# A gated mix of memory attention and a SwiGLU feed-forward block: stacks filled earlier, and part of the second half's input operands kept in DRAM

## The chip, the cores and the metric

The kernel runs on one core of one Trainium2 chip. Its time is the device time of one execution in microseconds (us). Several executions are timed, and the median is given; one more execution is recorded by the hardware profiler. The core's engines run side by side, each with an instruction stream of its own: TensorE (PE, with PEld for its weight loads), VectorE (DVE), ScalarE (ACT), GpSimd (POOL), and SyncE (SP), which issues nearly all DMAs.

## The reference

For x of 2048 tokens and D = 576 features the kernel computes one output:

```python
g = sigmoid((x * gate_w).sum(-1))
a = attention_with_memory(x, wq, wk, wv, wo, beta)   # 32 heads of 18, 4 segments of 512 tokens
b = (silu(x @ w_gate) * (x @ w_up)) @ w_down         # F = 4608
out = g * a + (1 - g) * b
```

In attention each segment of 512 tokens has causal softmax attention within itself, and a second part that reads a memory matrix per head, summed up over the segments before it: `num / den` of phi(q) with M and z, where phi(t) is t + 1 above zero and exp(t) below. The two parts are mixed by sigmoid(beta) of the head. Everything is float32 in the reference.

## The kernel before, in words

**Precision.** A float32 operand is split into a high part in TensorE's rounded format (`split`, L104: ScalarE copies, VectorE subtracts) and a low part, the remainder. A product is then three matmuls: high·high, high·low, low·high. An operand of two 128-row blocks is one tile of 128 × 2 × 512 floats, 512 KB, with high and low side by side.

**Stage 1, projections (L269 to L562).** Over four segments s of 512 tokens: nine chains for q and k (`qk`), then eight value steps n = 0 to 7 (`v_step`, with `mem_step` for the memory part). The x of a segment lives in tiles named `xo` plus `xs`; `xs_of[s]` holds the four split x tiles and the remainder of 64 rows. q and k go to DRAM (`stk`), the values to `vd`, the memory part to `med`. Those stores are first put into the list `late`; `flush` issues them some steps afterwards (L304, L527, L541, L558). In segment 3 the x sums of the feed-forward block's first half are made too (`first_load`, `first_sum`, `first_split`), and in its value steps the weight operands of unit 0 (`w_make`, list `start`).

**Feed-forward block, two halves.** Each half handles 1024 tokens as two column blocks (`HALF`: segments 2 and 3, then 0 and 1). A half has 36 units f of 128 rows of F. The gate and up products of a unit are combined into seven products of sums, as in Strassen's scheme: `seven(t, w[j], XO[j], ...)` with j = 0 to 6, weight operands w[j] and x operands XO[j]. XO[0], XO[3] and XO[5] are split parts of x itself; XO[1], XO[2], XO[4] and XO[6] are split sums or differences of x parts. `SLOT` says which `xo` tile pair holds operand j. Each j has two tiles, z = 0 and 1.

In half 0, `w_make` makes the weight operands (sums on POOL at L232, high parts on ScalarE at L236, low parts on VectorE at L239) and stores them to DRAM (`wc`, `rc`; L249 and L252). In half 1 `w_fetch` loads them back. There are only six operand tiles (pool `wop`): one comes free when its product is done and, in half 0, its store has landed.

**Order of the work.** The program is written in the order in which it is to run; each engine executes its own part in that order and waits where a tile is not ready. A unit has eight `tick`s; each calls `beat` (L870), which runs the front entry of the list `due` (deferred loads, sums, splits and stores, put there by `defer(k, ...)`, k beats ahead), then a number of down groups (`down_group`: products with w_down, added to `ya` on VectorE at L787), and, by a credit counter, steps of the attention generator `att_gen`. Between the halves ten extra beats (`BREAK`) run with the down groups of the last unit.

**Attention.** It works through 64 units u (two heads of a segment each), one after another, beside the feed-forward block. For each, `stack_load` (L179) loads stacked q and k rows from `stk` into `qst` and `kst` (four tiles each, in turn by u % 4), `s_bank` finds row maxima (L619, L626), `m_tr` transposes them to `mt`, stored to `mxd`; `row_load` (L195) loads three rows of it back into `qst`, and `t_bank` (L659, then the exponential on ScalarE, L663) uses them. Rows of kst beyond what is loaded must hold −1 (memsets at L602 and L604). The tiles qst, kst, mb and others lie in the pool `kp`, which is opened at L596, after stage 1, over memory that stage 1 used; the first write to it waits for the last reader of that memory.

**The second half's x.** `x_second` (L889) lists what prepares XO and XS of half 1: per z four loads of x parts into `raw` tiles (256 KB each, q = 0 to 3), four sums on POOL (`x_sum`, L153) and seven splits, plus the remainder of 64 rows for two blocks, loaded and split. Its numbers are beats counted from the first tick of the last unit of half 0 (f = 35): 0 to 7 are that unit's ticks, 8 on are the break's beats.

**Queues.** SP issues its DMAs strictly in program order. In the built program each DMA also waits until the eighth DMA before it has landed, since eight semaphores are used in turn. So a DMA whose data are late holds up all that stand behind it on SP.

Of the kernel before, what the change touches and what calls it, by code (L numbers as in the profile page):

```python
# [12 lines left out]
F32 = mybir.dt.float32  # L13
F32R = mybir.dt.float32r
BF = mybir.dt.bfloat16
# [5 lines left out]
P = 128  # L21
# [30 lines left out]
def f32(ap):  # L52
    return ap.bitcast(F32)
# [3 lines left out]
def gated_mix(ctx, tc, xT, wf, wd, wv, wo, beta, cmask, ident, bmask, out):  # L57
# [11 lines left out]
    mxd = dram.tile([2 * NB, 3, 8, P], BF, name="mxd")  # L69
    wc = dram.tile([FT, 7, P, 4 * P], F32, name="wc")  # L70
    rc = dram.tile([FT, 2, P, 2 * P], F32, name="rc")
    dc = dram.tile([FT, P, 2 * D], F32, name="dc")
    ffd = dram.tile([8, P, D], F32, name="ffd")
    atd = dram.tile([16, P, D], F32, name="atd")
# [29 lines left out]
    def split(hi, lo, src):  # L104
        nc.scalar.activation(hi, src, AF.Copy)  # L105
        nc.vector.tensor_sub(lo, src, f32(hi))  # L106
# [39 lines left out]
    def x_split(x, kt, raw):  # L146
# [2 lines left out]
            split(xk[kt][:, 0], xk[kt][:, 1], raw)  # L149
        else:  # L150
            xs_split(xs, raw)

    def x_sum(j, c, d, e, g):  # L153
        if j == 1:
            nc.gpsimd.tensor_sub(c, d, c)
        elif j == 2:
            nc.gpsimd.tensor_sub(c, g, c)
        elif j == 4:
            nc.gpsimd.tensor_sub(d, g, d)
        elif j == 6:  # L160
            nc.gpsimd.tensor_sub(e, e, c)

    spare = [(j, z) for j in (2, 3, 4) for z in range(2)]
    turns = iter(spare + [(j, z) for j in (5, 6) for z in range(2)] + 20 * spare)
# [104 lines left out]
    with ExitStack() as st:  # L269
        qst_ = ExitStack()  # L270
        qp = pool(qst_, "qp", 1, side="right")
        vp = pool(st, "vp", 1)
        sp = pool(st, "sp", 2)
        qw = []
        for m in range(5):
            qw.append([[qp.tile([P, NT, P], F32R, name=f"{z}{m}{u}") for u in range(2 if m < 4 else 1)] for z in ("qhi", "qlo")])
        vw = [vp.tile([P, 2, NT, 290], F32R, name=f"vw{hf}") for hf in range(2)]
        vf = vp.tile([P, 4, H, E], F32, name="vf")
        vps = [vp.tile([P, 4, 16, 3, E], BF, name=f"vps{hf}") for hf in range(2)]
        bm = vp.tile([P, NT, MW], BF, name="bm")  # L280
# [216 lines left out]
        for s in range(NSEG):  # L497
            upd = upd_gen(s - 1) if s else None
            casts = []
            for n, (m, u) in enumerate(chains):  # L500
                mid = []
                if s == 0:
                    for z in loads.get(n, []):
                        z()
                    if n + 3 < 9:
                        mid.append(lambda n=n: q_split(*chains[n + 3]))
                    if n in halves:
                        mid.append(lambda n=n: v_split(*halves[n]))
                if s == 1 and n < 3:
                    cast = masks(*((0, 3), (3, NT), (0, 0))[n])  # L510
                    casts.append(cast)
                if s == 1 and 3 <= n < 6:
                    mid.append(casts[n - 3])
                if (s, n) == (1, 7):
                    mid.append(betas)
                if s == 3:
                    if 2 <= n < 6:
                        first_load(n - 2)
                    for j, z in FSUM.get(n, []):
                        mid.append(lambda j=j, z=z: first_sum(j, z))  # L520
                    for j, z in FSPLIT.get(n, []):
                        mid.append(lambda j=j, z=z: first_split(j, z))
                if s < 3:
                    for kt in ((0, 1), (2, 3), (4,))[n - 6] if s == 0 and n > 5 else (n - 4,) if s and n > 3 else ():
                        raws["x", kt] = x_load(s + 1, kt)
                qk(s, m, u, mid)
                flush(2)  # L527
                if upd is not None and n > 0:
                    next(upd, None)
            if s == 3:  # L530
                qst_.close()
                rp = pool(ctx, "rp", 4, side="right")
                wop = pool(ctx, "wop", 6, side="right")
                for z in range(2):
                    for j, b, kt in ((0, 2, z), (3, 2, 2 + z), (5, 3, 2 + z)):
                        XO[j][z] = xs_of[b][0][kt]
                wraw_of[0] = [w_load(0, u) for u in range(2)]
                start = w_make(0)
            for n in range(8):
                hf, i = divmod(n, 4)  # L540
                flush()  # L541
                v_step(s, hf, i)
                if s:
                    mem_step(s, n // 2, n % 2)
                if s < 3:
                    if n == 0:
                        xs_of[s + 1] = x_tiles(s + 1)
                    if 1 <= n < 6:
                        x_split(xs_of[s + 1], n - 1, raws["x", n - 1])
                else:  # L550
                    if n == 4:
                        wraw_of[1] = [w_load(1, u) for u in range(2)]
                    if n < 2:
                        first_sum(6, n)
                    for _ in range((0, 0, 2, 3, 3, 3, 3, 3)[n]):
                        if start[0][0] < 8:
                            start.pop(0)[1]()
# [7 lines left out]
    with ExitStack() as st:  # L565
# [12 lines left out]
        def row_tile():  # L578
            return rw.tile([P, L], F32, name="row")
# [15 lines left out]

        kp = pool(ast, "kp", 2, side="right")  # L596
        ap = pool(ast, "ap", 2, side="right")
        for i in range(NST):
            qst.append(kp.tile([P, 2, L], BF, name=f"qst{i}", bufs=1))
            kst.append(kp.tile([P, 2, L], BF, name=f"kst{i}", bufs=1))  # L600
            if i:
                defer(2 * i - 1, lambda i=i: nc.gpsimd.memset(kst[i], -1.0))  # L602
            else:
                nc.gpsimd.memset(kst[i], -1.0)  # L604
        for i in range(2):
            mbs.append(kp.tile([P, P], F32, name=f"mb{i}", bufs=1))
            nc.gpsimd.memset(mbs[i], 0.0)
        for pr in range(2):
            stack_load(0, pr)
        SPLAN = [[(0, 0, 3)], [(0, 1, 3)], [(384, 0, 0), (0, 0, 2)], [(384, 1, 0), (0, 1, 2)], [(0, 0, 1), (256, 1, 1)]]  # L610

        def s_bank(u, n):
# [100 lines left out]
        def att_gen():  # L713
            N = 10 * NB
            for tau in range(N + TL + VL + 4):
# [4 lines left out]
                    nc.sync.dma_start(mxd[u - 1].rearrange("z q n -> q z n"), mts.pop(u - 1))  # L720
                if n == 0 and 2 <= u <= 2 * NB + 1:
                    row_load(u - 2)
                if n in (2, 3) and u + 1 < 2 * NB:
                    stack_load(u + 1, n - 2)
                z = tau - TL - VL - 1
                if z % 20 == 0 and 0 <= z < N and z // 20 + 1 < 4 * NSEG:
# [161 lines left out]

        def x_second(new, xs):  # L889
            r = {}  # L890

            def load(z, q):
                b, kt = ((0, z), (1, z), (0, 2 + z), (1, 2 + z))[q]
                r[z, q] = raw_tile()[:, :L]
                nc.sync.dma_start(r[z, q], xT[HALF[1][b], :, kt])

            def total(z, j):
                x_sum(j, *(r[z, q] for q in range(4)))

            def parts(z, j):  # L900
                new[j][z] = x_slot(SLOT[j], z)
                split(new[j][z][:, 0], new[j][z][:, 1], r[z, (0, 0, 0, 2, 1, 3, 2)[j]])

            def rest_load(b):
                r[b] = row_tile()
                nc.sync.dma_start(r[b], xT[HALF[1][b], :, 4])

            def rest(b):
                xs[b] = xs_tile()
                xs_split(xs[b], r[b])  # L910

            todo = []
# [26 lines left out]
        for pos, (half, f) in enumerate(seq):  # L939
# [176 lines left out]
```

## Time and profile before

| what | value |
|---|---|
| median of 3 runs | 1901.21 us (1895.81 to 1901.78) |
| the profiled execution | 1899.41 us, of which its span 1897.60 |
| mean granted TensorE clock | 0.993 of full |
| TensorE busy | 1822.3 us |
| VectorE, ScalarE, GpSimd busy | 1222.2, 961.5, 856.1 us |
| DMA traffic | 330.83 MB, mean 174 GB/s |

Stages in the trace: projections to 224 us, half 0 from there to about 1000, the break to 1034, half 1 to about 1800, the output product to 1898. The profile's tables are read like this: a group's line gives the source line, the engine, the operation and the tiles (out<-in); an instruction's line in a timeline begins with its start and its duration in us, and ends in square brackets with the time its engine sat idle before it and what ended that. A window's line gives the stretch, its length, then the busy time of PE, PEld, DVE, ACT and POOL with their numbers of instructions, the granted clock, the busy share of the DMA engines and GB/s. A wait's line names the waiting instruction, what it waited for, us in total, how many times, and the longest.

### The profile page before, as it was taken

The page shows a single profiled execution, that of the slowest core. Times are in us where ns is not written, and L with a number is a line of the kernel's source. Part 1 is how long each engine was busy: PE and PEld are TensorE (multiplying, and loading weights), DVE is VectorE, ACT ScalarE, POOL GpSimd, SP SyncE. Part 2 cuts the span into 40 slices and gives each one's busy share as a digit, 9 for nine tenths or more (in the row PEclk, how much of TensorE's full clock was granted, in tenths as well). Part 3 has the DMA queues.
Part 4 walks back from the last instruction along what each step waited for, and adds up shares of the span by engine and source line. Part 5 has one row for each costly group of instructions (what it writes and reads, how often), then busy time and mean ns, then how long its engine had stood idle before and what let it go on. Part 6 is the DMA issues. An engine that isn't in the chain of part 4 may idle for free.

```text
span 1897.6 us, 36543 instructions
## 1 busy us (share of the span) xinstructions
PE 1822.3 (96%) x12508; PEld 1546.4 (81%) x12508; DVE 1222.2 (64%) x3034; ACT 961.5 (51%) x1786; POOL 856.1 (45%) x1246
## 2 busy tenths in 40 slices
PE   8999989999999999999998999999999999999999
PEld 7889867877877887887787788878878878888899
DVE  5555666777767777876777565656556555655455
ACT  7666545466456556645654544554454444355311
POOL 3323622455544555555455444445454444445121
PEclk9999989999999999999999999999999999999999
DMA  6444485466456447645646644554554354445544
GB/s 226 157 143 167 156 277 193 147 230 205 140 195 230 158 161 239 212 153 188 221 156 209 205 150 119 186 160 129 160 180 149 122 177 148 140 151 156 191 149 138
DMA packets 204457, 330.83 MB, mean 174 GB/s; under 512 B 38192, under 2 KB 95664, under 8 KB 204272
## 3 DMA queue, kind: packets, MB, share of 16 engines
q1 hardware_dynamic: 204272, 328.50, 53.0%
q8 instruction: 100, 1.64, 0.4%
q14 instruction: 85, 0.70, 0.1%
HBM read 194.33 MB, written 134.09 MB: 173 GB/s over the span
## 4 chain that ended last, share of the span: by engine, by line
PE 77%; DVE 6%; DMA 6%; ACT 5%; issue 4%; SPq 2%; POOL 1%; DVEq 0%; ACTq 0%; POOLq 0%
PE bank L927 26%; PE bank L782 23%; PE bank L128 11%; PE bank L933 5%; PE bank L619 3%; PE bank L659 3%; PE bank L688 2%; PE bank L690 1%; ACT L663 1%; PE bank L369 1%; DMA draw<-in_wd_dram 1%; ACT pe L663 1%; ACT L1001 1%; PE bank L415 1%; SPq L189 1%
## 5 line engine op out<-in xcount | busy, mean ns | idle before, releaser
L738 POOL TENSOR_TENSOR p<-pe,p 128x512 f16<-128x512 f32 x320 | 372.8, 1165 | 692.0 <-DVE p L736 608.0
L782 PE MATMUL bank<-dw,hh 128*128 128x288 f32 x2304 | 484.4, 303 | 18.6 <-DVE ya L787 12.9
L782 PEld LDWEIGHTS bank<-dw,hh 128*128 128x128 f32 x2304 | 380.3, 190 | 41.4 <-DVE ya L787 19.7
L663 ACT ACTIVATE pe<-bank 128x512 f32<-128x512 f32 x320 | 191.0, 597 | 339.2 <-PE bank L659 301.2
L782 PE MATMUL bank<-dw,hl 128*128 128x288 f32 x1152 | 341.4, 296 | 1.5 <-DVE hl L106 1.5
L787 DVE TENSOR_TENSOR ya<-bank,ya 128x288 f32<-128x288 f32 x352 | 159.7, 455 | 229.4 <-PE bank L782 227.3
L626 DVE CUSTOM_DVE_ANT_0 scr<-bank,cm 128x512 bf16<-128x512 f32 (+3 forms) x512 | 246.9, 482 | 18.6 <-PE bank L619 11.8
L782 PEld LDWEIGHTS bank<-dw,hl 128*128 128x128 f32 x1152 | 218.1, 189 | 1.9 <-DVE hl L106 1.9
L659 PE MATMUL bank<-qst,kst 111*128 111x512 bf16 (+3 forms) x512 | 152.1, 305 | 0.0
L736 DVE CAST p<-pe 128x512 f16<-128x512 f32 x320 | 150.1, 469 | 1.0 <-POOL pe L671 0.9
L671 POOL TENSOR_SCALAR_AFFINE_SELECT pe<-pe 128x256 f32<-128x256 f32 (+1 forms) x320 | 135.9, 425 | 15.3 <-ACT pe L663 13.6
L619 PE MATMUL bank<-kst,qst 108*128 108x512 bf16 (+3 forms) x512 | 126.8, 301 | 13.5 <-ACT pe L663 13.4
L1008 DVE TENSOR_TENSOR bank<-bank,row 128x512 f32<-128x512 f32 x72 | 50.3, 698 | 106.5 <-ACT row L1004 105.9
L995 ACT ACTIVATE row<-bank 128x512 f32<-128x512 f32 x72 | 43.0, 597 | 130.1 <-PE bank L933 129.7
L663 ACT ACT_TABLE_LOAD x66 | 84.7, 1283 | 46.7 <-PE bank L659 43.9
L106 DVE TENSOR_TENSOR hl<-row,hh 128x512 fp32r<-128x512 f32 x72 | 51.2, 711 | 81.9 <-ACT hh L105 81.9
L128 PE MATMUL bank<-xo,qhi 128*128 128x512 f32 x288 | 92.7, 403 | 5.3 <-ACT xo L105 5.2
L659 PEld LDWEIGHTS <-kst 111*128 111x128 bf16 x512 | 48.0, 98 | 53.1 <-issue 38.4
L999 ACT ACTIVATE bank<-bank 128x512 f32<-128x512 f32 x72 | 41.9, 582 | 92.4 <-PE bank L927 87.4
L1001 ACT ACT_TABLE_LOAD x67 | 86.0, 1283 | 1.2
L325 POOL TENSOR_TENSOR q<-qr,q 128x512 bf16<-128x512 f32 x36 | 43.8, 1217 | 93.4 <-ACT q L324 84.1
L984 ACT ACTIVATE bank<-bank 128x512 f32<-128x512 f32 x72 | 42.0, 583 | 78.4 <-PE bank L927 68.4
(2091 smaller groups left out, 4250.2 us busy)
## 6 DMA issues: line engine op xcount, KB each, us to landing
raw<-in_wf_dram SPq DMA_DIRECT2D x72, 320.0 KB
dc<-dw SPq DMA_DIRECT2D x36, 576.0 KB
dw<-dc SPq DMA_DIRECT2D x36, 576.0 KB
stk<-q SPq DMA_DIRECT2D x32, 384.0 KB
draw<-in_wd_dram SPq DMA_DIRECT2D x36, 288.0 KB
vd<-vps SPq DMA_DIRECT2D x8, 912.0 KB
v<-vd SPq DMA_DIRECT2D x16, 456.0 KB
qst<-stk SPq DMA_DIRECT2D x128, 54.0 KB
```

The lines of the kernel that those rows point to most:

```text
L128: nc.tensor.matmul(t, st[n], mv[n], start=(n == 0), stop=(n == 13))
L619: nc.tensor.matmul(t[:, c:c + w], qs[:KR, pr, P * i:P * i + P], ks[:KR, pr, 0:w], start=True, stop=True)
L626: nc.vector.tensor_tensor_reduce(scr[:, :w], t[:, c:c + w], cm[:, L - w:L], 1.0, -3.0e38, OP.add, OP.max, m[:, k:k + 1])
L659: nc.tensor.matmul(t[:, c:c + w], ks[:KR + 3, pr, P * j:P * j + P], qs[:KR + 3, pr, P * j:L], start=True, stop=True)
L663: nc.scalar.activation(pe, t, AF.Exp, scale=SCALE)
L671: nc.gpsimd.affine_select(d, d, pattern=pat, compare_op=OP.is_ge, fill=0.0, base=0, channel_multiplier=-1)
L736: nc.vector.tensor_copy(p1, pe)
L738: nc.gpsimd.tensor_sub(p2, pe, p1)
L782: nc.tensor.matmul(t, p, q[:, cs], start=(n == 0), stop=(n == 3 * CH - 1))
L787: nc.vector.tensor_add(ya[:, i, cs], t, ya[:, i, cs])
L927: nc.tensor.matmul(t, w[:, p, z], x[z][:, q], start=first and n == 0, stop=last and n == 5, skip_group_check=True)
L1001: nc.scalar.activation(sg0, sg0, AF.Silu)
```

## The change

It has two parts.

**Stacks.** The tiles qst and kst move to a pool of their own, `kq`, opened during stage 1 when its query pool `qp` has closed. The memsets of kst move into value steps 2 to 5 of segment 3, and the stack loads of attention units 0 and 1 into value steps 4 to 7 (one `stack_load` call in each); attention unit 0 no longer loads the stack of unit 1. The value weights `vw` get a pool of their own below `vp`, so that other tiles of the feed-forward block lie over `vw` than before.

**The second half's x.** Two new DRAM tiles, `xd` and `xsd`, take the split x parts of segments 0 and 1 that are operands 0, 3 and 5 of half 1 (six tiles), and both remainders. They are stored through `late` in the value steps of segments 0 and 1. `x_second` loads these back (`kept`, and `rest` without a split). For the other four operands it still loads raw x parts, sums on POOL and splits; the loads, sums and splits are placed on earlier beats, the sums partly in other tiles (as `first_sum` does). `x_sum` is gone. Of the break's ten beats the second now has no down groups either, as the first.

```diff
+    xd = dram.tile([2, 4, P, 2 * L], F32, name="xd")
+    xsd = dram.tile([2, P, L], F32, name="xsd")
...
-    def x_sum(j, c, d, e, g):
-        if j == 1:
-            nc.gpsimd.tensor_sub(c, d, c)
-        elif j == 2:
-            nc.gpsimd.tensor_sub(c, g, c)
-        elif j == 4:
-            nc.gpsimd.tensor_sub(d, g, d)
-        elif j == 6:
-            nc.gpsimd.tensor_sub(e, e, c)
...
+        vwp = pool(st, "vwp", 1)
         vp = pool(st, "vp", 1)
...
-        vw = [vp.tile([P, 2, NT, 290], F32R, name=f"vw{hf}") for hf in range(2)]
+        vw = [vwp.tile([P, 2, NT, 290], F32R, name=f"vw{hf}") for hf in range(2)]
...
                 wop = pool(ctx, "wop", 6, side="right")
+                kq = pool(ast, "kq", 1, side="right")
+                for i in range(NST):
+                    qst.append(kq.tile([P, 2, L], BF, name=f"qst{i}"))
+                    kst.append(kq.tile([P, 2, L], BF, name=f"kst{i}"))
...
                 if s:
                     mem_step(s, n // 2, n % 2)
+                if s < 2 and n > 1 and n - 2 in ((0, 1, 2, 3), (2, 3))[s]:
+                    late.append((xd[s, n - 2], f32(xs_of[s][0][n - 2]).rearrange("p a b -> p (a b)")))
+                if s < 2 and n == 6:
+                    late.append((xsd[s], f32(xs_of[s][1])))
...
                     if n < 2:
                         first_sum(6, n)
+                    elif n < 6:
+                        nc.gpsimd.memset(kst[n - 2], -1.0)
+                    if n > 3:
+                        stack_load(n // 2 - 2, n % 2)
...
-        for i in range(NST):
-            qst.append(kp.tile([P, 2, L], BF, name=f"qst{i}", bufs=1))
-            kst.append(kp.tile([P, 2, L], BF, name=f"kst{i}", bufs=1))
-            if i:
-                defer(2 * i - 1, lambda i=i: nc.gpsimd.memset(kst[i], -1.0))
-            else:
-                nc.gpsimd.memset(kst[i], -1.0)
...
-        for pr in range(2):
-            stack_load(0, pr)
...
-                if n in (2, 3) and u + 1 < 2 * NB:
+                if n in (2, 3) and 0 < u < 2 * NB - 1:
                     stack_load(u + 1, n - 2)
...
             def total(z, j):
-                x_sum(j, *(r[z, q] for q in range(4)))
+                c, d, e, g = (r[z, q] for q in range(4))
+                o, p, q = {1: (c, d, c), 4: (d, g, d), 2: (g, g, c), 6: (e, e, g)}[j]
+                nc.gpsimd.tensor_sub(o, p, q)
 
             def parts(z, j):
                 new[j][z] = x_slot(SLOT[j], z)
-                split(new[j][z][:, 0], new[j][z][:, 1], r[z, (0, 0, 0, 2, 1, 3, 2)[j]])
...
+                split(new[j][z][:, 0], new[j][z][:, 1], r[z, {1: 0, 4: 1, 2: 3, 6: 2}[j]])
+
+            def kept(z, j):
+                b, kt = {0: (0, z), 3: (0, 2 + z), 5: (1, 2 + z)}[j]
+                new[j][z] = x_slot(SLOT[j], z)
+                nc.sync.dma_start(f32(new[j][z]).rearrange("p a b -> p (a b)"), xd[b, kt])
 
             def rest(b):
                 xs[b] = xs_tile()
-                xs_split(xs[b], r[b])
...
-            for z, loads, at in ((0, ((0, 3), (1, 3), (3, 4), (2, 5)), 9), (1, ((0, 12), (1, 13), (3, 13), (2, 14)), 14)):
-                todo += [(o, lambda z=z, q=q: load(z, q)) for q, o in loads]
-                for o, j, what in ((0, 0, parts), (0, 1, total), (1, 1, parts), (1, 2, total), (1, 3, parts),
-                                   (2, 2, parts), (2, 4, total), (2, 6, total), (3, 4, parts), (3, 5, parts),
-                                   (4, 6, parts)):
-                    todo.append((at + o, lambda z=z, j=j, what=what: what(z, j)))
-            for b in range(2):
-                todo += [(10, lambda b=b: rest_load(b)), (17 + b, lambda b=b: rest(b))]
+                nc.sync.dma_start(f32(xs[b]), xsd[b])
+
+            for z, loads, sums, splits in ((0, (0, 1, 5, 4), (6, 6, 7, 7), (8, 8, 9, 10)),
+                                           (1, (9, 9, 11, 10), (12, 12, 13, 13), (13, 14, 14, 15))):
+                todo += [(o, lambda z=z, q=q: load(z, q)) for o, q in zip(loads, range(4))]
+                for o, p, j in zip(sums, splits, (1, 4, 2, 6)):
+                    todo += [(o, lambda z=z, j=j: total(z, j)), (p, lambda z=z, j=j: parts(z, j))]
+                todo += [(o + z, lambda z=z, j=j: kept(z, j)) for o, j in ((2, 0), (6, 3), (8, 5))]
+            todo += [(11 + b, lambda b=b: rest(b)) for b in range(2)]
...
-                        beat(None if n else 0)
+                        beat(None if n > 1 else n)
```

More of the change, by code (lines that the diff above doesn't have):

```diff
@@ L890, in x_second @@
             r = {}
+            todo = []
             def load(z, q):
@@ L897, in total @@
             def total(z, j):
-                x_sum(j, *(r[z, q] for q in range(4)))
+                c, d, e, g = (r[z, q] for q in range(4))
+                o, p, q = {1: (c, d, c), 4: (d, g, d), 2: (g, g, c), 6: (e, e, g)}[j]
+                nc.gpsimd.tensor_sub(o, p, q)
             def parts(z, j):
                 new[j][z] = x_slot(SLOT[j], z)
-                split(new[j][z][:, 0], new[j][z][:, 1], r[z, (0, 0, 0, 2, 1, 3, 2)[j]])
-            def rest_load(b):
-                r[b] = row_tile()
-                nc.sync.dma_start(r[b], xT[HALF[1][b], :, 4])
+                split(new[j][z][:, 0], new[j][z][:, 1], r[z, {1: 0, 4: 1, 2: 3, 6: 2}[j]])
@@ L908, in rest @@
+            def kept(z, j):
+                b, kt = {0: (0, z), 3: (0, 2 + z), 5: (1, 2 + z)}[j]
+                new[j][z] = x_slot(SLOT[j], z)
+                nc.sync.dma_start(f32(new[j][z]).rearrange("p a b -> p (a b)"), xd[b, kt])
             def rest(b):
                 xs[b] = xs_tile()
-                xs_split(xs[b], r[b])
-            todo = []
-            for z, loads, at in ((0, ((0, 3), (1, 3), (3, 4), (2, 5)), 9), (1, ((0, 12), (1, 13), (3, 13), (2, 14)), 14)):
-                todo += [(o, lambda z=z, q=q: load(z, q)) for q, o in loads]
-                for o, j, what in ((0, 0, parts), (0, 1, total), (1, 1, parts), (1, 2, total), (1, 3, parts),
-                                   (2, 2, parts), (2, 4, total), (2, 6, total), (3, 4, parts), (3, 5, parts),
-                                   (4, 6, parts)):
-                    todo.append((at + o, lambda z=z, j=j, what=what: what(z, j)))
```

## The prediction

> **What bounds the kernel now.** I read the busy shares first, then windows over the two stretches that the edit touches, then their waits and timelines.
>
> ```profile
> span 1897.6 us, 36543 instructions
> ...
> PE 1822.3 (96%) x12508; PEld 1546.4 (81%) x12508; DVE 1222.2 (64%) x3034; ACT 961.5 (51%) x1786; POOL 856.1 (45%) x1246
> ```
> ```profile
> 5.00:224.00 219.00, 216.83 (x1277) 194.91 (x1278) 125.64 (x302) 136.58 (x273) 84.82 (x92) 1.00 0.48 167
> 224.00:250.00 26.00, 16.35 (x63) 11.79 (x63) 11.23 (x30) 11.92 (x28) 7.72 (x12) 0.86 0.69 245
> 1000.00:1034.00 34.00, 27.43 (x204) 24.83 (x203) 27.07 (x55) 11.44 (x20) 21.32 (x23) 0.90 0.61 213
> 1034.00:1800.00 766.00, 749.05 (x5445) 624.09 (x5444) 447.42 (x1184) 357.42 (x580) 352.43 (x550) 1.00 0.51 157
> ```
>
> TensorE bounds: 1822.3 of 1897.6 us. In the windows (length, busy time of PE, PEld, DVE, ACT, POOL, clock, DMA share, GB/s) the two stretches that the edit rearranges are the poor ones: 9.65 of 26 us idle after the projections ("the start"), 6.57 of 34 between the halves ("the break"), both below full clock. The stage 5–224 is 99% busy.
>
> ```profile
> PE bank L927 <- DVE row L1012: 6.7, 1, 6.7
> ```
> ```profile
> 227.75 0.32 SPq L306 DMA_DIRECT2D med<-om  x1
> 231.35 0.85 SPq L187 DMA_DIRECT2D qst<-stk  x1
> ...
> 239.75 0.41 SPq L249 DMA_DIRECT2D wc<-wo__2428  x1
> ```
> ```profile
> 231.50 0.95 POOL L604 MEMSET kst<- 128x1024 bf16 x1 [5.28 <-DMA med<-om]
> ...
> 234.49 0.73 POOL L232 TENSOR_TENSOR ws<-raw 128x256 f32<-128x256 f32 x1
> ```
> ```profile
> 235.25 0.42 ACT L236 ACTIVATE wo__2600<-ws 128x256 fp32r<-128x256 f32 x1 [0.93 <-POOL ws L232]
> ...
> 245.64 0.42 ACT L236 ACTIVATE wo__2616<-ws 128x256 fp32r<-128x256 f32 x1 [7.55 <-DMA wc<-wo__2428]
> ```
> ```profile
> 238.88 1.66 PE L927 MATMUL bank<-xo,wo__2588 128*128 128x512 f32 x6 [1.17 <-DVE bank L1008]
> 247.27 2.90 PE L927 MATMUL bank<-xo,wo__2600 128*128 128x512 f32 x6 [6.72 <-DVE row L1012]
> ```
>
> The start: the last `med` store, issued 227.75, lands 231.22; POOL's first memset in the new pool and, behind it, the weight sums of unit 1 wait for that. SP spends 231.35–238.4 issuing ten stack loads, so the store wc<-wo__2428, which frees an operand slot, goes out at 239.75 and lands at 245.58. ScalarE waits 7.55 us for it, VectorE's queue behind that, TensorE 6.72.
>
> ```profile
> PE bank L782 <- DVE ya L787: 4.4, 3, 2.3
> PE bank L782 <- ACT hh L105: 1.1, 1, 1.1
> PE bank L782 <- DVE hl L106: 1.0, 1, 1.0
> PE bank L927 <- DVE bank L991: 1.0, 1, 1.0
> ```
> ```profile
> 1001.41 0.63 ACT L105 ACTIVATE hh<-row 128x512 fp32r<-128x512 f32 x1
> ...
> 1006.62 0.63 ACT L105 ACTIVATE xo<-raw 128x512 fp32r<-128x512 f32 x1 [0.20 <-DMA raw<-in_xT_dram]
> ```
> ```profile
> 1000.06 0.78 SPq L895 DMA_DIRECT2D raw<-in_xT_dram  x1
> ...
> 1001.55 0.33 SPq L895 DMA_DIRECT2D raw<-in_xT_dram  x1
> ...
> 1004.26 0.27 SPq L195 DMA_DIRECT2D qst<-mxd  x1
> ```
>
> The break: TensorE waits 2.1 us for the first hh/hl and 4.4 us on ya adds that stand on VectorE behind xo splits. Granted clock was .50 in 1004–1006 and .67 in 1006–1008 (1.67 us lost), and .89/.50/.75 over 1016–1022 (1.72 lost). DMA is .93 to .99 busy from 992 to 1004 at some 320 GB/s; the raw load issued at 1001.55 landed at 1006.6, five microseconds for 256 KB.
>
> **The change part by part.**
>
> *Writes of x parts in the projections.* Eight stores are added: six operands at 512 KB and two remainders at 256 KB, 3.5 MB, in segments 0 and 1 (36–150 us). At 400 GB/s 9 us of DMA in a stage at DMA share .48, in SP's queue among stores that nothing on TensorE waits for. Cost taken 0, cover: the 52% free DMA time. Bounds −0.5 to +1.5 (one x or weight load landing late; largest gap in that stage is the 2.17 us that 219 us leave idle in all).
>
> *Memsets into value steps.* 4 × 0.95 on POOL, 16.1 of 24 us busy in 200–224: fits, 0. vw in a pool of its own lets the first row tile overlay vp alone: the p5 copy (L987) waited 2.73 us for vd<-vps. That wait goes, and TensorE's 0.93 with it; but unit 0's gain ends at the same later stall, so I count nothing.
>
> *Stack loads of units 0 and 1 ahead of the end.* Twenty issues instead of ten before the end, and none in attention unit 0. In the built program SP meets, after vd at 218.33: med, two raws, stack loads, wc stores, the last med and vd. At the trace's issue times (0.85, .73, .62, .60, .31, .29 for six, .71, .72, .62, .61 for four) these are 6.0 + 6.1 us for both units' sets; each waits for the eighth before it. So the last med goes out at about 236.4 instead of 227.75, and lands 3.47 us later (as before) at about 240. POOL's mb memset still opens the pool that waits for it; the weight sums go from 234.49 to about 240.7, unit 1's second high from 235.25 to about 241.9, and with the table load, silu, L1004 and L1008 behind it (3.6 us as before) unit 1's first product from 238.88 to about 245.5. The counterpart of wc<-wo__2428 goes out behind v and draw at about 241.7 instead of 239.75 (+1.9). So the second product starts at about 249.0 instead of 247.27. Of this 1.8 I take back 1.2: the first product, run just ahead, takes the slow-clock time (2.90 against 1.66 in the rows). **Start +0.6**, bounds +3 (landing 2.4 us later behind the moved loads) and −3 (med landing early because DMA was light in 230–240: 56 GB/s).
>
> The loads gone from attention unit 0 (270.38 on, 3.3 us of SP) had nothing waiting: 0.
>
> *Six splits fewer.* Six times 0.62 (ScalarE) and 0.68 (VectorE) and two xs splits leave the break; six loads of 512 KB and two of 256 come instead of two row loads: 3.1 MB net, 7.9 us at 400 GB/s, in 993–1012 where DMA is full.
>
> *Sums and splits earlier.* The built program's order on ScalarE in the break's first beat: the exponential, the split of sum 1, the split of sum 4, and only then hh; before, hh stood first (1001.41). Sum 4 reads the third load, issued at tick 4 as before (1000.06) but with two 512 KB loads ahead of it in place of two 256 KB ones that moved up. From 992 about 4.46 MB are ahead of it; at .32 MB/us and 1.5 us of latency it lands at about 1007. Then 1.27 (POOL), 0.63 (ScalarE): hh at about 1009, first down group some 7 us late (+7). After that the break is lighter: the ya waits go (−3.4 of 4.4), the second clock drop (−1.7), the attention work moved ahead of the wait (−0.6), the L991 wait (−1.0), giving +0.3; with the landing 1 us later +1.3: taken 1.3. The two down groups that the break's second beat gives up only move to later beats.
>
> *The query-row load* (L195). Issued 1004.26 before, first used by TensorE at 1012.04. After, it waits for the eighth DMA before it, the third x load, so is issued at or after 1007, behind 2.6 MB where 1.6 MB stood. At 400 GB/s it lands between 1010.5 and 1014, and TensorE's attention product after the first group wants it at 1010.5: 0 to +3.5. No row is nearer to one end; I take the middle, 1.75. The five-us landing above shows that a load waits out what was issued ahead of it. The Trainium skill, "DMA: Bandwidth & Descriptors" (section "Queues, rings and completion order"), says the same as a rule: SP's copies share one row of rings, and each DMA engine consumes descriptors in ring order. By the rule alone the small load would stand behind all 2.6 MB and the term would be 3.5, not 1.75.
>
> **Break** 1.3 + 1.75 = **+3.05**, bounds −6.7 (hh not delayed) to +8.
>
> Sum: 1899.41 (the profiled execution, 1897.60 of it span) + 0.6 + 3.05 = 1903.1. The median of the runs, 1901.21, stands 1.8 above that execution; half of it added gives **1904.0**, likeliest by itself 1899.5 to 1907.
>
> **Rivals.**
>
> *Slower: ring order.* The row load waits for all kept operands (+1.75 more), the third x load lands at 1009 instead of 1007 (+2), and the longer wait at half clock costs more (.50 over 244–252 after the 6.72 us wait, with 4.73 busy: 2.4 lost, against 1.67: +0.7). 1904 + 4.45 = 1908.5. For it: the DMA share of .98 before a byte is added. Against: packets of loads issued later went among others in 1006–1008 at 412 GB/s.
>
> *Faster: operands arrive in time.* If the third x load lands by 1003, sum, split and hh are ready by about 1005 behind products that TensorE has anyway; then +3.05 is replaced by −3.4 − 1.7 − 1.0 − 0.6 = −6.7: 1894.2. It decides at a landing of about 1006, above which the late hh costs more than the lighter break gives. For it: two raw loads moved to the unit's first ticks. Against: the rate of 320 GB/s in 992–1004.
>
> *The start stall vanishes.* If med lands in time and an operand slot is free by 241, the 6.72 go: 1904 − 0.6 − 6.7 = 1896.7. Against: the store that frees the slot still stands behind v and draw.
>
> **How the numbers follow.** Forecast .38, ring order .37, operands in time .18, start stall gone .05, both good ones together .02 (1887). About 0.3% (5.7 us) is what a measurement of this kernel tells from no change: slower begins at 1906.9, faster ends at 1895.5. So slower .37, faster .20, same .43. The range 1893.5 to 1911 takes in the centres of the first three cases and the start case, and leaves out the double gain, the lower part of the third and the far end of the second (together about .18).
>
> **What would show it.** Start: the last med issued near 236, POOL's mb memset waiting for it, the first product of unit 1 near 245.5 and the second near 249. Break: ScalarE's first hh after two xo splits near 1009, a TensorE wait of 6 to 8 us on it, then ya waits under 1 us and a clock of 1.00 over 1016–1022; the attention product after group 1 waiting for qst<-mxd or not. Wrong if hh goes at 1002–1004, if the wait on DVE row L1012 is gone, or if the projections' 99% falls.

## The result, and the profile after

The changed kernel takes 1903.99 us, median of 20 runs (1901.52 to 1908.60), beside 1900.19 us for the kernel before, median of 20. The medians lie 3.8 apart, the means of the same runs (1904.66 and 1899.74) 4.9. The ratio is 1.0026, 95% interval 1.0019 to 1.0033, which is 4.9 us of 1900: slower by less than 0.3%, but clear of no change. The forecast was 1904.0. The profiled execution took 1903.28 us, its span 1901.6, which is 4.0 more than before.

The windows of the same stretches in the changed kernel (length, then busy time of PE, PEld, DVE, ACT and POOL, clock, DMA share, GB/s):

```profile
5.00:224.00 219.00, 217.50 (x1279) 195.24 (x1280) 126.09 (x302) 136.78 (x272) 87.79 (x95) 1.00 0.52 183
224.00:250.00 26.00, 11.79 (x50) 8.67 (x48) 8.80 (x23) 8.57 (x19) 4.83 (x9) 0.81 0.49 173
1000.00:1034.00 34.00, 22.52 (x155) 19.43 (x153) 21.31 (x41) 12.05 (x21) 20.89 (x22) 0.75 0.84 303
1034.00:1800.00 766.00, 752.61 (x5492) 627.83 (x5490) 446.35 (x1186) 353.23 (x571) 352.23 (x550) 1.00 0.51 156
```

The two stretches that the edit rearranges have both become worse: TensorE is busy 11.79 of 26 us instead of 16.35 at the start, and 22.52 of 34 instead of 27.43 in the break. The projections are as before (217.50 of 219), with their DMA share up from .48 to .52. The second half is better, 13.39 us idle instead of 16.95. The waits of TensorE, first in the start, then in the break:

```profile
PE bank L925 <- DVE bank L1006: 12.5, 1, 12.5
```
```profile
PE bank L778 <- ACT hh L107: 7.4, 1, 7.4
PE bank L778 <- DVE hl L108: 1.5, 1, 1.5
...
PE bank L778 <- DVE ya L783: 0.9, 2, 0.5
PE bank L655 <- DMA qst<-mxd: 0.7, 1, 0.7
```

In place of 6.7 us on row L1012 stands one wait of 12.5 us; in place of 2.1 on hh/hl and 4.4 on ya stand 8.9 and 0.9. Equal products in the two profiles show where the difference arises (before, after, difference so far): the first product of unit 0 at 223.75 and 223.41 (−0.3); of unit 2, when the start is over, at 260.31 and 263.83 (+3.5); the last seventh product of half 0 at 997.79 and 1000.72 (+2.9); the first product of the third unit of half 1, when the break is over, at 1063.15 and 1069.63 (+6.5); the end at 1897.6 and 1901.6 (+4.0). So up to unit 2 the change has cost 3.5, the break costs 3.55, and the units that follow each are shorter by 0.6 and 2.5. These two last figures are no more than the profiles of this case differ by in such stretches: from the silu (the sigmoid-weighted copy on ScalarE, `row<-row`, one per unit) of unit 3 to that of unit 34, the two kernels and the twelve runs below take 696.7 to 700.6 us (697.6 before, 697.3 here), and from that of the third unit of half 1 to the end 815.5 to 822.5 us (822.0 before, 818.9 here). That the change gives time back there is not shown.

**The start.** SyncE, GpSimd, ScalarE and TensorE of the changed kernel, one view each:

```profile
237.86 0.34 SPq L299 DMA_DIRECT2D vd<-vps  x1
238.30 0.37 SPq L299 DMA_DIRECT2D med<-om  x1
244.93 0.62 SPq L191 DMA_DIRECT2D v<-vd  x1
245.63 0.56 SPq L203 DMA_DIRECT2D draw<-in_wd_dram  x1
246.25 0.42 SPq L241 DMA_DIRECT2D wc<-wo__2472  x1
```
```profile
245.18 0.35 POOL L605 MEMSET mb<- 128x128 f32 x2 [18.44 <-DMA med<-om]
245.49 0.72 POOL L224 TENSOR_TENSOR ws<-raw 128x256 f32<-128x256 f32 x1
```
```profile
246.25 0.42 ACT L228 ACTIVATE wo__2627<-ws 128x256 fp32r<-128x256 f32 x1 [11.46 <-POOL ws L224]
...
250.95 0.42 ACT L228 ACTIVATE wo__2643<-ws 128x256 fp32r<-128x256 f32 x1 [1.85 <-DMA wc<-wo__2472]
```
```profile
249.88 2.93 PE L925 MATMUL bank<-xo,wo__2616 128*128 128x512 f32 x6 [12.47 <-DVE bank L1006]
252.61 2.04 PE L925 MATMUL bank<-xo,wo__2627 128*128 128x512 f32 x6
```

The vd store's data were ready by 226.74, when POOL's last L344 ended; it goes out at 237.86, because SyncE is issuing stack loads until then. The med store behind it lands only at 244.8; POOL's memset waits for that, the weight sums stand behind the memset, and ScalarE's second high part behind the sums. The operand store wc<-wo__2472 stands behind v, which waits for the same med.

**The break.** ScalarE, SyncE and the clock:

```profile
1004.10 0.62 ACT L107 ACTIVATE xo<-raw 128x512 fp32r<-128x512 f32 x1
1011.81 0.63 ACT L107 ACTIVATE xo<-raw 128x512 fp32r<-128x512 f32 x1 [7.09 <-POOL raw L897]
1012.35 0.61 ACT L107 ACTIVATE hh<-row 128x512 fp32r<-128x512 f32 x1
```
```profile
1004.41 0.39 SPq L892 DMA_DIRECT2D raw<-in_xT_dram  x1
...
1010.40 0.27 SPq L187 DMA_DIRECT2D qst<-mxd  x1
```
```profile
1010.00:1014.00 4.00, 0.85 (x2) 0.50 (x2) 1.53 (x2) 2.00 (x4) 3.33 (x3) 0.50 1.05 400
1014.00:1018.00 4.00, 1.95 (x7) 1.50 (x8) 4.00 (x5) 2.06 (x5) 3.57 (x4) 0.50 1.03 409
1018.00:1020.00 2.00, 1.83 (x8) 1.48 (x7) 2.00 (x5) 0.00 (x0) 1.92 (x3) 0.50 1.04 400
1020.00:1022.00 2.00, 1.64 (x7) 1.64 (x8) 1.90 (x7) 0.00 (x0) 1.85 (x5) 0.50 0.53 191
1022.00:1024.00 2.00, 2.00 (x10) 2.00 (x10) 0.46 (x1) 0.00 (x0) 1.92 (x5) 0.50 0.77 238
1024.00:1026.00 2.00, 2.00 (x14) 2.00 (x12) 0.46 (x1) 0.00 (x0) 1.92 (x2) 0.76 0.67 195
```

hh stands on ScalarE behind the split of sum 4, whose third x load was issued at 1004.41; hh starts 11.6 us after the last seventh product of half 0 (1000.72); in the kernel before it was 3.6 us after it. The query row, which TensorE wants next, was issued at 1010.40. The granted clock falls to .50 at 1007.9, during the wait for hh, and is back at 1.00 only at 1025.0.

### The profile page after: what moved, and what is told of

It reads as the page before. It is cut to its first block, busy times and chain, and to the rows that moved or that the text cites. A ratio compares the mean times of both kernels' runs of the same rounds, so it can differ in the third digit from the quotient of the medians.

```text
span 1901.6 us, 36530 instructions
## 1 busy us (share of the span) xinstructions
PE 1820.7 (96%) x12508; PEld 1543.4 (81%) x12508; DVE 1217.8 (64%) x3026; ACT 958.1 (50%) x1778; POOL 856.6 (45%) x1246
## 4 chain that ended last, share of the span: by engine, by line
PE 76%; DVE 7%; DMA 6%; ACT 5%; issue 3%; SPq 1%; POOL 1%; ACTq 0%; DVEq 0%; POOLq 0%
PE bank L925 25%; PE bank L778 23%; PE bank L130 11%; PE bank L931 5%; PE bank L655 3%; PE bank L615 3%; PE bank L684 2%; DMA raw<-in_wf_dram 1%; PE bank L686 1%; ACT L659 1%; DMA woraw<-in_wo_dram 1%; DMA draw<-in_wd_dram 1%; PE bank L362 1%; ACT hh L107 1%; ACT pe L659 1%
```

## The experiments

All differences are given as the ratio to the kernel before on the same chip, less one, times 1900 us; the changed kernel stands at +4.9 (3.6 to 6.3). Differences between two runs are taken from their ratios too, so the last digit can be off by one from the rounded values. On the two chips that served the experiments the kernel before took 1898.0 to 1898.8, so the absolute times in the expectations lie about 2 us too high. Line numbers differ by a few between versions.

**Each part alone.** First the stacks without the second-half part (the edit in words):

```text
 (kernel before)
+        vwp, kq, early memsets, stack_load(n // 2 - 2, n % 2) in value steps 4 to 7, 0 < u in att_gen
         x_second, x_sum, break as before; no xd, xsd
```

> The stack part alone on the kernel before (own pool for qst and kst, memsets and stack loads in the last value steps, vw in a pool of its own); x_second as before. Theory (each part loses in its own stretch): the second product of unit 1, 247.27 before and 252.61 after the change, stands at about 252 to 253 here, and the time is 1900.2 + 3 = about 1903. Rival (the start is late because of the added x stores or by chance): second product near 247, time about 1900.

Then the second-half part without the stacks (the edit in words):

```text
 (kernel before)
+        xd, xsd and their stores; the new x_second; beat(None if n > 1 else n)
         kq, vwp, stack loads as before
```

> The second-half part alone on the kernel before (x stores in segments 0 and 1, loads of kept operands, earlier sums); stacks as before. Theory: start as before (second product of unit 1 near 247.3), first hh of the break behind the split of sum 4, a TensorE wait of about 7 us on it, unit 2 of half 1 about 3.5 us later than before, some of it given back later: time 1900.2 + 1 to 3.5 = 1901 to 1904. Rival (the loss is all of the start, the break is even): 1900 or below.

Measured: the stacks alone 1900.56 us, ratio 1.0009 (1.0000 to 1.0018), +1.7; the second-half part alone 1898.47 us, ratio 1.0002 (0.9992 to 1.0012), +0.4 (−1.5 to 2.3), where +1 to +3.5 was expected: in the time the rival (the break is even) came nearer, though the waits are those of the theory. With the stacks alone the wait of the start was 12.4 us, the second product of unit 1 stood at 251.97 and unit 2 began at 263.35, 3.0 later than before. With the second-half part alone the start was as before (246.18), and the break had these waits:

```profile
PE bank L778 <- ACT hh L107: 6.8, 1, 6.8
PE bank L778 <- DVE hl L108: 1.5, 1, 1.5
PE bank L778 <- DVE ya L783: 1.2, 3, 0.7
```

So the wait on hh is there with and without the stacks. Its break, from the last seventh product of half 0 (997.15) to the third unit of half 1 (1064.47), is 2.0 longer than before (997.79 to 1063.15), where I expected 3.5, and half 1 has less idle time: 12.88 us in 1034 to 1800 instead of 16.95, as the changed kernel has 13.39. That this comes from the change is not shown, for the reason given above. The two parts add up to +2.1 where both together measure +4.9; with these intervals (the upper ends add up to 5.7) no interaction is shown, and neither is it shown that the two account for the whole.

**The start: is it POOL's wait for med?** In the changed kernel the mb tiles go where qst and kst are:

```diff
+                for i in range(2):
+                    mbs.append(kq.tile([P, P], F32, name=f"mb{i}"))
...
                         nc.gpsimd.memset(kst[n - 2], -1.0)
+                        if n > 3:
+                            nc.gpsimd.memset(mbs[n - 4], 0.0)
...
-        for i in range(2):
-            mbs.append(kp.tile([P, P], F32, name=f"mb{i}", bufs=1))
-            nc.gpsimd.memset(mbs[i], 0.0)
```

> The changed kernel with the two mb tiles in the pool of qst and kst and their memsets in value steps 4 and 5, so that POOL's weight sums of unit 1 no longer stand behind a memset that waits for the last med store. Theory (two things are late: POOL by med, and the operand stores that stand on SP behind v and draw): POOL's sums near 228 instead of 245.5, the first product of unit 1 near 239 instead of 249.9, but the second still near 251 to 252 behind the operand store issued near 246, time 1904 - 1 = about 1903. Rival (the wait of POOL alone makes the stall): second product near 241, time about 1904 - 9 = 1895.

Measured: 1905.37 us, ratio 1.0039 (1.0024 to 1.0055), +7.4. POOL's first sum of unit 1 ran at 226.41 and the first product at 242.28, but the next one waited:

```profile
242.28 2.93 PE L926 MATMUL bank<-xo,wo__2616 128*128 128x512 f32 x6 [4.96 <-DVE bank L1007]
252.35 2.90 PE L926 MATMUL bank<-xo,wo__2627 128*128 128x512 f32 x6 [7.14 <-DVE row L1011]
```

One wait of 12.5 had become two of 5.0 and 7.1, with both products at 2.9 us. So POOL's wait is real and not the bound; the operand store is late next, as expected; the time, expected 1 us below the changed kernel, did not fall. That this run is slower than the changed kernel is not shown: the intervals overlap.

**The start: is it the order on SyncE?** The last vd and med ahead of the stack loads of attention unit 1:

```diff
-                    if n > 3:
-                        stack_load(n // 2 - 2, n % 2)
+                    if n in (4, 5):
+                        stack_load(0, n % 2)
...
         flush()
+        for pr in range(2):
+            stack_load(1, pr)
```

> The changed kernel with the last vd and med stores issued ahead of the ten stack loads of attention unit 1 instead of behind them. Theory (the start is late because those stores stand behind the stack loads on SP): last med issued near 228 instead of 238.3, POOL's mb memset near 232 instead of 245.2, the operand store behind v and draw near 236 instead of 246, the second product of unit 1 near 243 to 244 (252.6 in the changed kernel, 247.3 before): the time falls by 5 to 9 against the changed kernel, to or just under the kernel before. Rival (SP is not the cause, the landing of the stores in a full DMA is): second product near 250, time unchanged.

The same with mb early and v later (`defer(4, lambda: v_fetch(0))`):

> As the run with the stores first, and the mb tiles in the pool of qst and kst with early memsets, and the first v load four beats later, so that neither POOL nor the operand stores wait for the last med store. Theory: operand store near 234.5, first product of unit 1 near 239, second near 240 to 242, TensorE waits in 224 to 250 about 4 instead of 13 to 14; another 2 us below the run with the stores first. Rival (the wait then moves to the next late thing, draw or the raw loads): second product as in that run, same time as that run.

Measured: 1901.43 us, ratio 1.0012 (1.0003 to 1.0021), +2.3, and 1900.25 us, ratio 1.0012 (1.0002 to 1.0023), +2.3. The start is as before the change, not better: the second product of unit 1 at 249.10 and at 247.17. Both expectations had the operand store too early, and the time with it: the first run was to gain 5 to 9 on the changed kernel and gained 2.6, the second was to gain another 2 and gained nothing that can be told. SyncE reached vd only at 231.27 and 230.31, behind the stack loads of unit 0, and the operand store at 241.70 and 240.48, behind those of unit 1. In the second of them nothing of POOL was late any more, and the store alone held everything up:

```profile
240.48 0.34 SPq L241 DMA_DIRECT2D wc<-wo__2470  x1
```
```profile
245.55 0.42 ACT L228 ACTIVATE wo__2643<-ws 128x256 fp32r<-128x256 f32 x1 [8.29 <-DMA wc<-wo__2470]
```

So the store itself has to move. The next run takes, besides mb and v as above, the stack loads of unit 1 back to attention unit 0 and the first w_down load to a later tick:

```diff
-                if n in (2, 3) and 0 < u < 2 * NB - 1:
+                if n in (2, 3) and u < 2 * NB - 1:
...
-                    if (q, k) in ((0, 0), (1, 3), (2, 1)):
+                    if (q, k) in ((0, 0 if f else 4), (1, 3), (2, 1)):
```

> The changed kernel with, at the start: mb tiles early, the stack loads of attention unit 1 back in attention unit 0, the first v load four beats later, the first w_down load at tick 4 instead of 0. So the operand store that frees a slot stands right behind the last vd and med on SP. Theory (the wait of the start ends with that store: it goes out behind ten stack loads near 240.5 in the two runs with the stores first and takes 5 us): store near 231.5, landed by 236 to 237, second product of unit 1 near 239.5 to 241 instead of 252.6, TensorE waits of 224 to 250 about 3: the start 11 to 12 below the changed kernel, of which in the time 7 to 10. Rival (the store lands late whatever its place, DMA being full from 228 on): second product at 245 or later, time within 3 of the run with the early mb and the stores first.

Measured: 1894.16 us, ratio 0.9974 (0.9961 to 0.9987), −4.9, which is 9.9 below the changed kernel. Its SyncE, ScalarE and TensorE:

```profile
231.90 1.21 SPq L241 DMA_DIRECT2D wc<-wo__2470  x1
```
```profile
238.31 0.42 ACT L228 ACTIVATE wo__2633<-ws 128x256 fp32r<-128x256 f32 x1 [0.67 <-DMA wc<-wo__2470]
```
```profile
238.43 1.65 PE L926 MATMUL bank<-xo,wo__2604 128*128 128x512 f32 x6 [1.20 <-DVE bank L1007]
239.94 1.63 PE L926 MATMUL bank<-xo,wo__2617 128*128 128x512 f32 x6
```

The store goes out at 231.90, the second product starts at 239.94, and the stall of both kernels is gone. The first product of unit 2 stands at 254.89, 8.9 before that of the changed kernel.

**The break: what if hh stands ahead of the splits?**

```diff
-            for z, loads, sums, splits in ((0, (0, 1, 5, 4), (6, 6, 7, 7), (8, 8, 9, 10)),
+            for z, loads, sums, splits in ((0, (0, 1, 5, 4), (6, 6, 7, 7), (9, 9, 10, 10)),
```

> The changed kernel with the splits of the sums of z = 0 one or two beats later (9, 9, 10, 10 in place of 8, 8, 9, 10), so that hh stands ahead of them on ScalarE. Theory (hh is late because it stands behind a split that waits for the third x load): the wait of 7.4 us on hh goes to about 1, the break's clock drop of 1004 to 1012 shrinks, ya waits of 1 to 3 us come back in part: 1904 - 4 to 6 = 1898 to 1900. Rival (TensorE then waits as long for something else of the full DMA, the query-row load or VectorE): 1902 to 1904.

Measured: 1902.88 us, ratio 1.0023 (1.0014 to 1.0032), +4.4: no gain that can be told from none. hh was no longer waited for, but TensorE now waited for the query row:

```profile
PE bank L655 <- DMA qst<-mxd: 9.5, 1, 9.5
```

The row load of 6 KB was issued at 1011.78, and the product that needs it started at 1017.47. In the changed kernel the same lateness lay hidden behind the wait on hh, where only 0.65 us of it showed. The theory did not hold, its rival did.

**The break: the 512 KB loads later.**

```diff
-                todo += [(o + z, lambda z=z, j=j: kept(z, j)) for o, j in ((2, 0), (6, 3), (8, 5))]
+                todo += [(o + z, lambda z=z, j=j: kept(z, j)) for o, j in ((6, 0), (9, 3), (12, 5))]
```

> The changed kernel with the loads of the six kept operands four beats later (6, 9, 12 and one more for z = 1, instead of 2, 6, 8), behind the raw x loads of z = 0. Theory (the late hh and the late query-row load both come from the 512 KB loads ahead of them): third x load issued near 1002 and landed near 1006, hh near 1007.5 instead of 1012.35, the wait on hh 3 to 4 us instead of 7.4, the wait for the query row under 1: time 2 to 4 below the changed kernel. Rival (the x load and the row are late because SP and its eight places are full, whatever the order): wait on hh 6 to 7, time unchanged.

Measured: 1899.73 us, ratio 1.0011 (1.0002 to 1.0020), +2.1, so 2.9 below the changed kernel. The wait on hh fell from 7.4 to 4.6 us and the wait for the row was 1.0. So 2.8 of the 7.4 came from the 1 MB that had been placed ahead of the raw loads, a little less than expected (3 to 4 us were to be left of the wait).

**Three edits together** (start with the stores first and mb early, kept operands later, hh first):

> The changed kernel with the three edits together: the start edits of the run before this one but one, kept operands later, and the splits of the sums behind hh. Theory (the stretches add up): second product of unit 1 at 240 to 242, waits on hh and on the query row 1 to 3 us each; time 8 to 12 below the changed kernel and 4 to 8 below the kernel before. Rival (what is gained at the start or in the break is given back in the units that follow): 0 to 3 below the kernel before.

Measured: 1896.45 us, ratio 0.9991 (0.9978 to 1.0005), −1.7, not told apart from the kernel before; 4 to 8 below it was expected. The time is in the rival's range, but not by its mechanism, for the gains were not made in the first place. The start was that of the run with mb early and the stores first (second product at 246.71), and the row load, issued 1006.34, was waited for until 1012.79:

```profile
1012.79 0.58 PE L658 MATMUL bank<-qst,kst 111*128 111x512 bf16 x1 [7.56 <-DMA qst<-mxd]
```

**The break: groups ahead of the row.** Kept operands later, hh first, and the second beat of the break with its two down groups again:

```diff
-                        beat(None if n > 1 else n)
+                        beat(None if n else 0)
```

> The changed kernel with, in the break: kept operands later, splits of the sums behind hh, and down groups in the second beat again, so that two of them stand ahead of the attention product that needs the query row. Theory (the row load is late by what SP and the DMA engines have ahead of it, and only work that TensorE has meanwhile covers it): waits on hh and hl about 2.5, on the query row 3 to 5 instead of 7.6 to 9.5: 3 to 5 below the changed kernel. Rival (the groups then wait for something else, ya or hl, as long): time as with the kept operands later alone.

Measured: 1899.08 us, ratio 1.0002 (0.9991 to 1.0012), +0.4, so 4.6 below the changed kernel, as expected (3 to 5). The waits are other ones than expected. The row is not waited for at all; in its place TensorE waits 3.3 us for a ya add that stands on VectorE behind the split of sum 4:

```profile
1008.99 1.20 DVE L108 TENSOR_TENSOR xo<-raw,xo 128x512 fp32r<-128x512 f32 x1 [2.13 <-ACT xo L107]
1010.11 0.45 DVE L783 TENSOR_TENSOR ya<-bank,ya 128x288 f32<-128x288 f32 x1
```

**Start and break together, and the row load earlier.** The edits of the last start run and of the last break run in one kernel:

> Both sets of edits, start and break, together. Theory: the two gains add, 9 to 14 below the changed kernel, 5 to 9 below the kernel before (ratio .995 to .998). Rival: part is given back in the units that follow, 2 to 4 below the kernel before.

And the same with every row load one attention step earlier:

```diff
-                if n == 0 and 2 <= u <= 2 * NB + 1:
-                    row_load(u - 2)
+                if n == 4 and 1 <= u <= 2 * NB:
+                    row_load(u - 1)
```

> As the run with both sets of edits, and every query-row load issued one attention step earlier, so that in the break it goes out ahead of the raw x loads of z = 0 and the kept operands. Theory (the row is late by its place on SP and behind the bytes ahead): the wait for it in the break falls under 1 us, time 2 to 4 below the run without this edit. Rival (the row load now stands waiting on SP for its store and holds up the loads behind it, in the break or in every unit): same or slower.

Measured: 1891.60 us, ratio 0.9961 (0.9945 to 0.9976), −7.4, and 1891.94 us, ratio 0.9966 (0.9952 to 0.9980), −6.5. Most of the two gains add (−9.9 and −4.6 against the changed kernel; together −12.4), as expected. The earlier row load, issued at 991.40 instead of 1000.42, brings nothing where 2 to 4 us were expected, since the down groups already cover the row: TensorE does not wait for it without this edit either. So the change with these edits is 7.4 us faster than the kernel before (4.6 to 10.4), once the first w_down load, the first v load and half of the moved stack loads give way to the operand store, and the kept loads and the splits to the x loads and to hh. How much of the 7.4 is due to the change and how much to the later w_down and v loads and the early mb memsets is not shown: the kernel before was not run with these alone.

## Why the prediction was right, step by step

- *Projections, 0.* Right: busy 217.50 of 219 us, unit 0 begins 0.3 earlier.
- *The p5 wait goes, and is absorbed by the later stall.* Right: the p5 copy of unit 0 ran at 228.30 without waiting for vd.
- *Start +0.6, with an upper bound of +3.* Mis-sized, and beyond its bound: +3.5 by the first product of unit 2. The second product came 5.3 later than before (1.8 forecast), of which 1.8 was taken back up to unit 2 (1.2 forecast). The mechanism was the one described (med behind the stack loads, POOL behind med, the operand store behind v), and from ScalarE's second high part to the first product it took the 3.6 us of the forecast (246.25 to 249.88). Two terms failed. The med store was issued at 238.30, not 236.4. And "lands 3.47 us later (as before)" was taken from a row in which vd had gone out 1.5 us ahead of it; now 912 KB of vd went out 0.44 us ahead, and med landed 6.5 us after its issue. That the shorter distance to vd is what lengthened the landing is argued, not tested. The windows of that landing in the changed kernel show the end of it, with about an eighth of the DMA engines' time in use:

```profile
239.00:240.00 1.00, 0.00 (x0) 0.00 (x0) 0.00 (x0) 0.00 (x0) 0.00 (x0) 0.95 1.05 425
...
242.00:243.00 1.00, 0.00 (x0) 0.00 (x0) 0.00 (x0) 0.00 (x0) 0.00 (x0) 0.50 0.12 51
243.00:244.00 1.00, 0.00 (x0) 0.00 (x0) 0.00 (x0) 0.00 (x0) 0.00 (x0) 0.50 0.12 47
```

- *Break +3.05.* Right in sum: +3.55 by the third unit of half 1. Its terms: the first down group late by 7, measured 6.8 (hh 7.38 against 1.08, hl 1.53 against 1.02). The 1.5 us of latency in the landing of the third x load stands in no row that the forecast shows; its sum on POOL began at 1010.51, and half 0 had ended 2.9 later than before, so it landed by 1007.6 in the forecast's time, where about 1007 was said. The ya waits −3.4, measured −3.5. The L991 wait gone (−1.0), as said. The query row +1.75, measured +0.65. The second clock drop gone, −1.7: wrong, and in its sign. The clock was forecast at 1.00 over 1016 to 1022 and was .50, and it stayed there to 1025: busy 6.27 us at .50 between 1010 and 1022, 2.00 at .50 and 2.00 at .76 after that lose 4.6, against 1.67 + 1.72 before, so this term was worth +1.2. With these and the −0.6 for moved attention work, which was not measured, the terms give 6.8 − 3.5 − 1.0 + 0.65 + 1.2 − 0.6 = 3.55. The forecast was 2.9 too low on the clock; the 1.0 that it added for a later landing and 1.1 too much for the row made up most of that, so its sum is nearer than its terms.
- *The rival of ring order.* The time it gave, 1908.5, did not come. One of its parts did, the longer time at half clock (4.6 us lost instead of 3.4). The late row was there too, hidden: with hh out of the way the row was waited for 9.5 and 7.6 us. Issued at 1010.40 in the changed kernel, it released TensorE at 1016.65; 6.2 us at the 400 to 409 GB/s of those windows are 2.5 MB, close to the 2.6 MB that the prediction put ahead of it. On the rule of the Trainium skill, "DMA: Bandwidth & Descriptors" (section "Queues, rings and completion order"), that each DMA engine consumes the descriptors of a ring in order, these rows agree: the 6 KB came through only after about all that stood ahead.
- *The rival of the vanishing start stall* called for an operand slot free by 241 and said that the store stands behind v and draw. That was the right point: with the store moved from behind them and from behind the stack loads of unit 1, the stall went, and the time fell by 9.9.
- *The sum.* That 1904.0 meets 1903.99 is luck. In the two profiles the start's extra 2.9 and the 3.1 us by which the later units were shorter, for which no term stood, nearly cancel. And the base moved: the forecast started from a median of 1901.21, so it said +2.8, while the kernel before came out 1.0 lower and the change at +3.8 by the medians and +4.9 (3.6 to 6.3) by the ratio. What the working got right is the direction, the two stretches, and the chains that end last in them (med, POOL and the operand store; the third x load and hh).

## What to carry to other kernels

On a queue that issues in order, a transfer moved to an earlier place is paid for by all that it now precedes: look for the store on which a slot or a pool depends, and ask first whether that one goes out later. Behind a wait there can stand another of nearly the same length, so a fix of one (mb early, hh first) can show no gain until the next is covered too; give the engine work to cover it rather than only a new order. A landing time from a row holds only for what was ahead of that transfer in that row. A sum that comes out right is no proof of its terms: set each beside its own measurement.

## What was not expected of the hardware

From 242 on, the rest of the vd and med stores moved at about 50 GB/s with a DMA share of .12, while 239 to 242 had gone at 300 to 425 GB/s. The packet records of the trace show this rest as two chains of packets, in which each packet (7296 bytes in 0.28 us, later 2304 bytes in 0.09 us) starts as the one before it ends; the last packet of all others is over by 241.82, the last of these two chains at 244.34. So the landing waited for two chains out of many. In the kernel before, where vd and med had been issued 1.5 us apart, the chains that ended last were 0.3 us behind the others. Why two chains are late is not known here. And a load of 6 KB took 5.7 to 6.5 us from issue to the product that waited for it (1011.78 to 1017.47; 1006.34 to 1012.79) with the DMA engines .95 to 1.05 busy in the windows of those stretches.
